# One expert choice spread over more vector slots, its counts copied out of PSUM first, and a row load put in front of twelve weight loads

## The chip, the cores and the metric

The kernel runs on one core of a Trainium2 chip. The metric is the device time of the whole program in microseconds (us): the median of three runs before the change is 731.31 us, from 730.92 to 732.39. A profile shows one further execution, in which TensorE (PE, with its weight loads PEld), VectorE (DVE), ScalarE (ACT), GpSimd (POOL) and SyncE (SP, here a queue that issues DMAs) each work through instructions of their own in order, and wait for one another on semaphores.

## The reference

Three stages follow one another; each is fp32.

```python
# clustered attention: 2 batches, 8 heads, 768 tokens, 64 columns
mask = q_assign[:, :, :, None] == k_assign[:, :, None, :]
scores = np.where(mask, scale * np.matmul(q, k.transpose(0, 1, 3, 2)), -1e9)
attn = softmax(scores);  x = attn @ v              # -> (1536, 512)
# mixture of experts: 8 experts, one expert per token
e_idx = np.argmax(x @ w_gate, axis=1)
h = np.maximum(x[mask_e] @ w1[e], 0.0)
out[mask_e] = gate_w * sigmoid(x @ w_output_gate)[e] * (h @ w2[e])
# dense feed-forward, 512 -> 2048 -> 512
h = x @ w_in;  g = h * sigmoid(1.702 * h);  return g @ w_out
```

## The kernel before, in words

**Attention.** The work is cut into eight units, one for a batch and a pair of heads (batch 0 is units 0 to 3, batch 1 units 4 to 7), and each unit into 12 steps of 128 queries against 768 keys, so 96 steps in one loop over `i`. In iteration `i` the program issues, in this order: the scores of step `i+1` on PE (L515 and L516, four matmuls in a PSUM tile `sp`, of which there are two) and their maximum on DVE (L518, `nm`); the piece of output that is due (L586, `pox`); what a table puts at this `i` (`soon_at`, below); the products with v (L567, only in some iterations, which makes those steps longer); the six transposes of step `i-1` (L532, `pt`, two groups of three: the first copied out by ACT at L537, the second by DVE at L539); last, the exponential of step `i+1` on ACT (L524, `P`). The scores of a step need two tiles in a row to come free, a transpose needs `P`, and `P` needs `nm`: PE, DVE and ACT work in a loop.

**Routing of a batch.** `route(gi)` is a generator: after each group of three transposes the loop advances it by two `yield`s (`advance(2)`), so four in an iteration. `route(0)` handles the 768 tokens of batch 0 while units 5 to 7 run. It finds each token's expert; ranks the tokens within their expert with matmuls into the PSUM tile `prk` (L652 to L661); and puts in the same bank, as `part`, the number of tokens of each expert. From `part` it chooses one expert, the one with most tokens (`soonh`), and sets aside up to 128 of its tokens (`ngone`, `gone`); it derives from that the addresses `dest` of all rows, then a gate value, and sends the rows to DRAM: per tile, a scaling on POOL (L725, `xs`) and an indirect DMA of POOL (L730, `xd`), one tile in an iteration, six in all.

**The PSUM bank `m`.** The pool `ps_m` has one bank. `prk` lies in it, and so do `pox` (L586), the transposed q and k of the next unit (`pqk`, L337) and cluster scores (`pcl`, L418). The tile after `prk` can be written when the last reader of `prk` is done.

**The early expert work.** The chosen expert's 128 rows are worked off in plain fp32 while the routing is finished. `soon_ids` (L747) loads the expert's number and first row into registers of SP; `soon_weights` issues twelve weight loads on SP (L760, `ew`, nine of 384 KB, two of 256 and one of 128); `soon_rows` issues the load of the 128 rows (L782, `xs`), behind a wait for all six scatters; `soon_x` transposes them on PE (L790, `pxs`) in iteration 91, and the matmuls with the weights (L806, L816) come behind the loop, once route(2) begins. `soon_at` sets the iterations of these four; SP works through its queue in the order in which they are issued. POOL also cuts the next unit's q and k in two parts for the scores (L343 and L344: `Hq`, `Lq`, `Hk`, `Lk`), and SP copies these to where the scores read them (L362).

Of the kernel before, what the change touches and what calls it, by code (L numbers as in the profile page):

```python
# [14 lines left out]
ALU = mybir.AluOpType  # L15
# [8 lines left out]
E = 8  # L24
# [22 lines left out]
def attention_moe_ffn(ctx: ExitStack, tc: tile.TileContext, q, k, v, centroids, w_gate, w_og, w1, w2, w_in, w_out, out):  # L47
    nc = tc.nc
# [11 lines left out]
    rev8 = const.tile([128, E], F32, name="rev8")  # L60
    ebase = const.tile([128, E], F32, name="ebase")
# [17 lines left out]
    soon = const.tile([1, 2], I32, name="soon")  # L79
    gone = const.tile([128, E], F32, name="gone")  # L80
    ngone = const.tile([128, 1], F32, name="ngone")
    sbase = const.tile([128, E], F32, name="sbase")
    srev8 = const.tile([128, E], F32, name="srev8")
    span = const.tile([128, 3], F32, name="span")
    soonh = const.tile([128, E], F32, name="soonh")
# [460 lines left out]
    def queue_av(i):  # L546
# [33 lines left out]
        def ostage():  # L580
            n = len(heads)
            hh = 2 * pr + heads[0]
            po = ps_m.tile([128, 512], F32, name="pox", tag="m")
            pv = po[:, :3 * n * XW].rearrange("p (r h c) -> p r h c", r=3, h=n)
            for r in range(3):
                nc.tensor.matmul(pv[:, r], hold["oa"][:, r * 128:(r + 1) * 128], wl[:, 2 * pr + h] if alone else wo[:, pr], start=True, stop=True)  # L586
            scale = hold["rs"][:, heads[0]:heads[-1] + 1].rearrange("p h r -> p r h")
            nc.vector.tensor_tensor(xw[b][:, j0:j0 + 3, hh:hh + n, :], pv, scale[:, :, :, None].to_broadcast([128, 3, n, XW]), op=ALU.mult)
            if (pr, j0) == (H // 2 - 1, 0) and b == B - 1:
                routing.append(route(1))  # L590
# [15 lines left out]
    def route(gi):  # L606

        b, j0, nj = GROUPS[gi]
        js = slice(j0, j0 + nj)

        def new(nm, shape, dt=F32):
            return one.tile(shape, dt, name=f"{nm}{gi}")
# [37 lines left out]
        rk = pr[:, :nj * E].rearrange("p (t e) -> p t e", t=nj)  # L650
# [7 lines left out]
        if gi < len(GROUPS) - 1:  # L658
            part = pr[:, 256:256 + E]
# [6 lines left out]
        dest = new("dest", [128, nj, E])  # L666
        if gi < len(GROUPS) - 1:
            lk = new("lk", [128, E])
        if gi == 0:
            nc.vector.scalar_tensor_tensor(lk, part, float(E), rev8, op0=ALU.mult, op1=ALU.add)  # L670
            lm, lv = new("lm", [128, 1]), new("lv", [128, E])
            nc.vector.tensor_reduce(lm, lk, op=ALU.max, axis=AX.X)
            nc.vector.tensor_scalar(soonh, lk, lm, None, op0=ALU.is_equal)
            yield
            nc.vector.tensor_tensor(lv, soonh, part, op=ALU.mult)
            nc.vector.tensor_reduce(ngone, lv, op=ALU.add, axis=AX.X)
            nc.vector.tensor_scalar(ngone, ngone, float(FIRST), None, op0=ALU.min)
            yield
            nc.vector.tensor_scalar(gone, soonh, ngone, None, op0=ALU.mult)
            nc.vector.scalar_tensor_tensor(sbase, gone, -1.0, ebase, op0=ALU.mult, op1=ALU.add)  # L680
            nc.vector.scalar_tensor_tensor(srev8, gone, -float(E), rev8, op0=ALU.mult, op1=ALU.add)
            yield
            nc.vector.tensor_tensor(lv, soonh, ebase, op=ALU.mult)
            nc.vector.tensor_reduce(span[:, 1:2], lv, op=ALU.add, axis=AX.X)
            nc.vector.tensor_tensor(span[:, 0:1], span[:, 1:2], ngone, op=ALU.subtract)
            yield
            nc.vector.tensor_tensor(lv, soonh, iota8, op=ALU.mult)
            nc.vector.tensor_reduce(lm, lv, op=ALU.add, axis=AX.X)
            nc.vector.tensor_copy(soon[:, 0:1], lm[0:1])
            nc.vector.tensor_copy(soon[:, 1:2], span[0:1, 0:1])  # L690
        nc.vector.tensor_tensor(dest, rk, sbase[:, None, :].to_broadcast([128, nj, E]), op=ALU.add)
        if gi == len(GROUPS) - 2:
            nc.vector.scalar_tensor_tensor(lk, part, float(E), srev8, op0=ALU.mult, op1=ALU.add)
        yield
# [13 lines left out]
        if gi == len(GROUPS) - 2:  # L708
            lm, lv = new("lm", [128, 1]), new("lv", [128, E])
# [40 lines left out]
    def soon_weights():  # L750

        m1_ = w1[bass.ds(sooner["e"], 1)].rearrange("o (k p) f -> p (o k) f", p=128)
        m2_ = w2[bass.ds(sooner["e"], 1)].rearrange("o (i p) d -> p (o i) d", p=128)
        homes = [(ld, f"ld_{nm}", 4 if nm == "v" else 2) for nm in "qqkkvv"] + [(one, x + nm, 1) for x in "HL" for nm in "qk"] + [(one, "Fq", 1)]

        def tile_of(*parts):
            pool, tag, bufs = homes.pop(0)
            t = pool.tile([128, 3, 256], F32, name="ew", tag=tag, bufs=bufs)
            for n, src in parts:
                nc.sync.dma_start(out=t[:, n:n + src.shape[1]], in_=src)  # L760
            return t
        cols = [slice(256 * c, 256 * c + 256) for c in range(4)]
        for c in range(4):
            t = tile_of((0, m1_[:, 0:3, cols[c]]))
            for k in range(3):
                sooner[1, k, c] = t[:, k]
        t = tile_of((0, m1_[:, 3, 0:768].rearrange("p (c f) -> p c f", c=3)))
        for c in range(3):
            sooner[1, 3, c] = t[:, c]
        t = tile_of((0, m2_[:, 6:8, cols[0]]), (2, m1_[:, 3:4, cols[3]]))  # L770
        sooner[2, 6, 0], sooner[2, 7, 0], sooner[1, 3, 3] = t[:, 0], t[:, 1], t[:, 2]
        yield
        for x in range(2):
            for i0 in (0, 3, 6)[:2 if x == 0 else 3]:
                t = tile_of((0, m2_[:, i0:min(i0 + 3, 8), cols[x]]))
                for i in range(i0, min(i0 + 3, 8)):
                    sooner[2, i, x] = t[:, i - i0]
        yield
# [139 lines left out]
    slots.update({21: 3, 27: 1, 75: 1, 80: 1, 81: 2, 86: 3, 87: 2, 92: 2, 93: 2})  # L918

    weights = soon_weights()  # L920
    soon_at = {75: [soon_ids], 84: [lambda: next(weights)], 87: [lambda: next(weights), soon_rows], 91: [soon_x]}

    fixed = ExitStack()
    fixed.enter_context(tc.manual_schedule())
# [14 lines left out]
    for i in range(NS + 2):  # L939
# [16 lines left out]
        if i == NS // 2 + 13:  # L956
            routing.append(route(0))
# [24 lines left out]
    while ost:  # L982
        ost.popleft()()
    advance()
    routing.append(route(2))
    advance()
    finish_routing()
# [334 lines left out]
    with tc.manual_schedule():  # L1322
# [14 lines left out]
        for g in range(G + 2):  # L1337
# [24 lines left out]
            if g >= 2:  # L1362
                g0, ht = hq.popleft()
                e0, c0 = divmod(g0, 8)
# [128 lines left out]
```

## Time and profile before

| what | us |
|---|---|
| median of three runs | 731.31 (730.92 to 732.39) |
| the profiled execution | 733.72 |
| its span, first to last instruction | 732.0 |
| PE busy in the span | 703.2 (96%) |
| DVE busy | 458.1 (63%) |
| ACT busy | 393.0 (54%) |
| POOL busy | 264.4 (36%) |

The profiled execution's own time is 1.7 us above its span, which is what lies around the first and the last instruction, and 2.4 us above the median of the runs. Times in the rows count from the first instruction. An idle time in square brackets stands ahead of the instruction and names what ended it. [...]

### The profile page before, as it was taken

The page shows a single profiled execution, that of the slowest core. Times are in us where ns is not written, and L with a number is a line of the kernel's source. Part 1 is how long each engine was busy: PE and PEld are TensorE (multiplying, and loading weights), DVE is VectorE, ACT ScalarE, POOL GpSimd, SP SyncE. Part 2 cuts the span into 40 slices and gives each one's busy share as a digit, 9 for nine tenths or more (in the row PEclk, how much of TensorE's full clock was granted, in tenths as well). Part 3 has the DMA queues.
Part 4 walks back from the last instruction along what each step waited for, and adds up shares of the span by engine and source line. Part 5 has one row for each costly group of instructions (what it writes and reads, how often), then busy time and mean ns, then how long its engine had stood idle before and what let it go on. Part 6 is the DMA issues. An engine that isn't in the chain of part 4 may idle for free.

```text
span 732.0 us, 12543 instructions
## 1 busy us (share of the span) xinstructions
PE 703.2 (96%) x4522; PEld 580.2 (79%) x4522; DVE 458.1 (63%) x886; ACT 393.0 (54%) x789; POOL 264.4 (36%) x219
## 2 busy tenths in 40 slices
PE   8999999998999898999999897999999999999996
PEld 6776776776866678999999887888888888888885
DVE  6969788889888774344554545687655657232322
ACT  7767675675666544556777676544534344222120
POOL 2230330312750013755978889222432212020202
PEclk8999999999899999999999999999999999999999
DMA  6778969637274427766477776132643211010101
GB/s 195 171 189 266 238 216 293 142 121 173 69 200 141 174 86 255 230 215 215 161 254 243 236 224 222 59 116 86 68 73 41 81 59 56 1 58 1 58 0 58
DMA packets 70594, 105.18 MB, mean 144 GB/s; under 512 B 9648, under 2 KB 48304, under 8 KB 70528
## 3 DMA queue, kind: packets, MB, share of 16 engines
q1 hardware_dynamic: 67584, 95.94, 45.9%
q0 software_dynamic: 2944, 8.40, 3.0%
q8 instruction: 37, 0.61, 0.4%
q14 instruction: 29, 0.24, 0.1%
HBM read 70.46 MB, written 14.69 MB: 116 GB/s over the span
## 4 chain that ended last, share of the span: by engine, by line
PE 33%; issue 16%; ACT 5%; DVE 3%; POOL 2%; DMA 1%; POOLq 0%; ACTq 0%; DVEq 0%
PE ph L1317 4%; PE ph L1318 4%; PE ph L1319 4%; PE py L1412 3%; PE py L1411 3%; PE py L1410 3%; PE py L1134 3%; ACT w L1048 3%; PE ph L1134 3%; PE ph L1135 1%; PE py L1135 1%; DVE w L1051 1%; DMA raw<-in_moe_w_dram 1%; POOL out_dram L1421 1%; ACT hs L1140 1%
## 5 line engine op out<-in xcount | busy, mean ns | idle before, releaser
L1051 POOL TENSOR_TENSOR w<-raw,w 128x1024 fp32r<-128x1024 f32 x51 | 125.6, 2482 | 39.3 <-ACT w L1048 38.9
L518 DVE TENSOR_REDUCE nm<-sp 128x1 f32<-128x768 f32 x96 | 91.6, 955 | 16.2 <-PE sp L516 14.1
L1395 DVE TENSOR_TENSOR sg<-ph,sg 128x512 f32<-128x512 f32 x48 | 33.2, 691 | 99.7 <-ACT sg L1394 97.5
L524 ACT ACTIVATE P<-sp,nm 128x768 f32<-128x768 f32 x96 | 87.2, 908 | 11.3 <-DVE nm L518 10.6
L532 PEld LDWEIGHTS pt<-ident,P 128*128 128x128 f32 x576 | 66.4, 143 | 28.1 <-issue 17.5
L532 PE MATMUL pt<-ident,P 128*128 128x128 f32 x576 | 84.3, 280 | 4.0 <-ACT pT L537 2.1
L1394 ACT ACTIVATE sg<-ph 128x512 f32<-128x512 f32 x48 | 28.7, 597 | 104.7 <-PE ph L1319 100.3
L1134 PE MATMUL py<-ht,w 128*128 128x512 f32 (+6 forms) x224 | 70.2, 367 | 8.0 <-DVE ht L1158 5.1
L515 PE MATMUL sp<-X,Q 128*128 128x384 f32 x192 | 74.9, 390 | 0.5 <-ACT P L524 0.4
L1412 PE MATMUL py<-w,gl 128*128 128x512 f32 (+1 forms) x194 | 75.2, 387 | 0.0
L1411 PE MATMUL py<-w,gh 128*128 128x512 f32 (+1 forms) x194 | 75.1, 387 | 0.0
L1410 PE MATMUL py<-w,gh 128*128 128x512 f32 (+1 forms) x194 | 75.0, 387 | 0.0
L1317 PE MATMUL ph<-yth,w 128*128 128x512 f32 x192 | 74.8, 390 | 0.0
L1318 PE MATMUL ph<-ytl,w 128*128 128x512 f32 x192 | 74.7, 389 | 0.0
L1319 PE MATMUL ph<-yth,w 128*128 128x512 f32 x192 | 74.7, 389 | 0.0
L1084 POOL TENSOR_TENSOR w<-csq,w 128x512 fp32r<-128x512 f32 x24 | 32.7, 1364 | 115.7 <-ACT w L1083 115.7
L1048 ACT CAST w<-raw 128x1024 fp32r<-128x1024 f32 x68 | 70.5, 1042 | 4.2 <-issue 2.4
L1134 PE MATMUL ph<-t,w 128*128 128x512 f32 (+6 forms) x224 | 69.4, 365 | 0.4 <-DVE ht L1158 0.4
L567 PE MATMUL po<-pT,ld_v 128*32 128x384 f32 x768 | 69.0, 492 | 0.0
L516 PE MATMUL sp<-Z,Q 80*128 80x384 f32 x192 | 66.4, 346 | 0.5 <-DMA Q<-ohT 0.5
L537 ACT COPY pT<-pt 128x384 f32<-128x384 f32 x96 | 45.8, 477 | 36.8 <-PE pt L532 36.8
L539 DVE COPY pT<-pt 128x384 f32<-128x384 f32 x96 | 52.8, 550 | 12.6 <-PE pt L532 12.2
(291 smaller groups left out, 1476.2 us busy)
## 6 DMA issues: line engine op xcount, KB each, us to landing
raw<-in_moe_w_dram SPq DMA_DIRECT2D x64, 512.0 KB, 4.5
raw<-in_moe_w_in_dram SPq DMA_DIRECT2D x16, 512.0 KB, 4.1
raw<-in_moe_w_out_dram SPq DMA_DIRECT2D x16, 512.0 KB, 4.8
xd<-zrow SPq DMA_DIRECT2D x8, 768.0 KB, 5.9
Q<-Hq SPq DMA_DIRECT2D x28, 192.0 KB, 2.7
ew<-in_moe_w_dram SPq DMA_DIRECT2D x9, 384.0 KB, 7.8
ld_q<-in_q_dram SPq DMA_DIRECT2D x8, 384.0 KB, 6.0
ld_k<-in_k_dram SPq DMA_DIRECT2D x8, 384.0 KB, 3.8
```

Source lines behind the costliest of these rows:

```text
L518: nc.vector.tensor_reduce(nm, sp[:, :, :384], op=ALU.max, axis=AX.XY, negate=True)
L524: nc.scalar.activation(P, L["sp"][:, :, :384], AF.Exp, bias=L["nm"], accum_out=L["sm"][:, h, j % 3:j % 3 + 1])
L532: nc.tensor.transpose(pt[:, r * 128:(r + 1) * 128], L["P"][:, n, r * 128:(r + 1) * 128], ident)
L1048: nc.scalar.copy(hi, r)
L1051: (eng or nc.gpsimd).tensor_tensor(lo, r, f32(hi), op=ALU.subtract)
L1134: nc.tensor.matmul(ps[:, :2 * n], w_hi, t, start=first, stop=False)
L1317: nc.tensor.matmul(ph, wa(key, 0, k, i), yth[:, k, cs], start=(k == 0), stop=False)
L1318: nc.tensor.matmul(ph, wa(key, 0, k, i), ytl[:, k, cs], start=False, stop=False)
L1319: nc.tensor.matmul(ph, wa(key, 1, k, i), yth[:, k, cs], start=False, stop=(k == 3))
L1410: nc.tensor.matmul(po[m][:, cs], gh[:, ms], wb(key, 0, i)[:, cs], start=first, stop=False)
L1411: nc.tensor.matmul(po[m][:, cs], gh[:, ms], wb(key, 1, i)[:, cs], start=False, stop=False)
L1412: nc.tensor.matmul(po[m][:, cs], gl[:, ms], wb(key, 0, i)[:, cs], start=False, stop=last)
```

## The change

Three things change, all for the first batch's choice.

In `route(0)` the addresses are now formed first, from the ranks and the full table of first rows (`ebase`), and the counts `part` are copied into a tile `c0`; behind that nothing reads `prk`. The operations of the choice follow with a `yield` after nearly each one, where there were two or three between two `yield`s, and `gone` is taken off the addresses at the end. That adds two vector operations (the copy, and the subtraction on 128x48) and moves all that stands behind: the gates and the six scatters.

`soon_ids` moves from iteration 75 to 78, `soon_rows` from 87 to 84, where it stands in front of the first seven weight loads.

```diff
         if gi == 0:
-            nc.vector.scalar_tensor_tensor(lk, part, float(E), rev8, op0=ALU.mult, op1=ALU.add)
-            lm, lv = new("lm", [128, 1]), new("lv", [128, E])
+            nc.vector.tensor_tensor(dest, rk, ebase[:, None, :].to_broadcast([128, nj, E]), op=ALU.add)
+            lm, lv, c0 = new("lm", [128, 1]), new("lv", [128, E]), new("c0", [128, E])
+            nc.vector.tensor_copy(c0, part)
+            yield
+            nc.vector.scalar_tensor_tensor(lk, c0, float(E), rev8, op0=ALU.mult, op1=ALU.add)
+            yield
             nc.vector.tensor_reduce(lm, lk, op=ALU.max, axis=AX.X)
+            yield
             nc.vector.tensor_scalar(soonh, lk, lm, None, op0=ALU.is_equal)
             yield
-            nc.vector.tensor_tensor(lv, soonh, part, op=ALU.mult)
+            nc.vector.tensor_tensor(lv, soonh, c0, op=ALU.mult)
+            yield
             nc.vector.tensor_reduce(ngone, lv, op=ALU.add, axis=AX.X)
+            yield
...
+            nc.vector.tensor_tensor(dest, dest, gone[:, None, :].to_broadcast([128, nj, E]), op=ALU.subtract)
+        else:
+            nc.vector.tensor_tensor(dest, rk, sbase[:, None, :].to_broadcast([128, nj, E]), op=ALU.add)
...
-    soon_at = {75: [soon_ids], 84: [lambda: next(weights)], 87: [lambda: next(weights), soon_rows], 91: [soon_x]}
+    soon_at = {78: [soon_ids], 84: [soon_rows, lambda: next(weights)], 87: [lambda: next(weights)], 91: [soon_x]}
```

What PE and ACT are given, and in which order, stays the same. Three queues change their order. On DVE, before, from the scaled first rows `sbase` to the last reader of `prk`, which is L691:

```order
L680 SCALAR_TENSOR_TENSOR sbase<-gone,ebase 128x8
L681 SCALAR_TENSOR_TENSOR srev_76<-gone,rev_63 128x8
L683 TENSOR_TENSOR lv_2579<-soonh,ebase 128x8
L684 TENSOR_REDUCE span<-lv_2579 128x1
L685 TENSOR_TENSOR span<-span,ngone 128x1
L518 TENSOR_REDUCE nm<-sp 128x1
L687 TENSOR_TENSOR lv_2579<-soonh,iota_65 128x8
L688 TENSOR_REDUCE lm_2578<-lv_2579 128x1
L689 CAST soon<-lm_2578 1x1
L690 CAST soon<-span 1x1
L691 TENSOR_TENSOR dest_2575<-prk,sbase 128x48
L695 TENSOR_TENSOR dest_2575<-dest_2575,roh_85 128x48
```

Now, in the same place of the program, from the operation that stood ahead of the choice (L664) on:

```order
L664 TENSOR_REDUCE z_2572<-zz_2543 128x6
L670 TENSOR_TENSOR dest_2575<-prk,ebase 128x48
L672 COPY c_2580<-prk 128x8
L674 SCALAR_TENSOR_TENSOR lk_2576<-c_2580,rev_63 128x8
L539 COPY pT<-pt 128x3x128
L676 TENSOR_REDUCE lm_2578<-lk_2576 128x1
L678 TENSOR_SCALAR soonh<-lk_2576,lm_2578 128x8
L518 TENSOR_REDUCE nm<-sp 128x1
L680 TENSOR_TENSOR lv_2579<-soonh,c_2580 128x8
L682 TENSOR_REDUCE ngone<-lv_2579 128x1
L539 COPY pT<-pt 128x3x128
L684 TENSOR_SCALAR ngone<-ngone 128x1
```

The last reader of `prk` stood 20 rows behind L664 and is now the second row behind it; between two operations of the attention (L539, L518) stand two of the choice, where six stood.

On POOL, before, the end of the six scatters (`xs`, `xd`) and the parts of the last unit's q and k:

```order
L343 CAST Hq<-Fq 128x384
L344 TENSOR_TENSOR Lq<-Fq,Hq 128x384
L725 TENSOR_SCALAR xs<-xw_114,gate_2649 128x512
L730 DMA xd<-xs,di_2627 12416x512
L733 ISA
L343 CAST Hk<-Fk 128x384
L344 TENSOR_TENSOR Lk<-Fk,Hk 128x384
L343 CAST Hk<-Fk 128x384
L344 TENSOR_TENSOR Lk<-Fk,Hk 128x384
L176 DMA wd<-csq 128x512
```

Now, the same place:

```order
L343 CAST Hk<-Fk 128x384
L344 TENSOR_TENSOR Lk<-Fk,Hk 128x384
L741 TENSOR_SCALAR xs<-xw_114,gate_2758 128x512
L746 DMA xd<-xs,di_2712 12416x512
L749 ISA
L343 CAST Hk<-Fk 128x384
L344 TENSOR_TENSOR Lk<-Fk,Hk 128x384
L741 TENSOR_SCALAR xs<-xw_114,gate_2758 128x512
L746 DMA xd<-xs,di_2712 12416x512
L749 ISA
L741 TENSOR_SCALAR xs<-xw_114,gate_2758 128x512
```

Of the six scatters all stood ahead of the last three parts or further up, four of them ahead of the first; now one stands ahead of the first part and two stand behind the last.

On SP, before, the end of the weight loads and the row load:

```order
L760 ISA
L760 DMA ew<-in_moe_w_dram 128x2x256
L782 ISA
L782 DMA xs<-xd 128x512
L1006 TENSOR_LOAD lead
```

Now, the start of them, behind the rows of one-hots (`ohT`) for the last unit:

```order
L435 DMA Q_2780<-ohT 16x384 x2
L798 ISA
L798 DMA xs<-xd 128x512
L776 ISA
L776 DMA ew<-in_moe_w_dram 128x3x256
```

The row load stood behind all twelve weight loads and stands ahead of them. Further up SP, the register loads of `soon_ids` now stand behind the load `raw<-in_moe_w_out_dram` (L113) instead of ahead of it.

## Rows read from the trace of the kernel before

**Rows 1.** Stages: us, busy us (count) of each engine, granted clock, DMA share, GB/s.
```profile
171.75:191.39 19.64, 17.38 (x125) 12.91 (x123) 17.50 (x56) 9.69 (x23) 5.57 (x5) 0.83 0.39 102
206.88:222.03 15.15, 14.07 (x117) 10.11 (x116) 14.32 (x24) 9.45 (x21) 4.15 (x6) 1.00 0.70 192
```

**Rows 2.** Timeline of the choice: start, us, engine, line, names [idle before, releaser].
```profile
178.58 0.19 DVE L664 TENSOR_REDUCE z<-zz 128x6 f32<-128x48 f32 x1
...
179.80 0.55 DVE L539 COPY pT<-pt 128x384 f32<-128x384 f32 x1
...
180.31 0.81 PE L532 MATMUL pt<-ident,P 128*128 128x128 f32 x3 [1.01 <-ACT pT L537]
...
181.23 0.96 DVE L518 TENSOR_REDUCE nm<-sp 128x1 f32<-128x768 f32 x1
...
182.62 0.18 DVE L691 TENSOR_TENSOR dest<-prk,sbase 128x48 f32<-128x48 f32 x1
...
182.86 1.97 PE L586 MATMUL pox<-wo,oa 128*128 128x160 f32 x6 [0.45 <-DVE dest L691]
...
185.76 0.67 PE L515 MATMUL sp<-X,Q 128*128 128x384 f32 x1
```

**Rows 3.** Timeline of DVE behind the choice: its idle times, first and last.
```profile
186.15 0.56 DVE L539 COPY pT<-pt 128x384 f32<-128x384 f32 x1 [0.53 <-PE pt L532]
...
189.74 0.55 DVE L405 TENSOR_TENSOR oh<-eq,m 128x384 bf16<-128x384 f32 x1
...
196.03 0.96 DVE L518 TENSOR_REDUCE nm<-sp 128x1 f32<-128x768 f32 x1 [0.22 <-PE sp L516]
```

**Rows 4.** Timeline of POOL: scatters and parts.
```profile
185.74 1.57 POOL L725 TENSOR_SCALAR xs<-xw,gate 128x512 f32<-128x512 f32 x1 [8.02 <-DVE gate L707]
...
188.78 1.58 POOL L725 TENSOR_SCALAR xs<-xw,gate 128x512 f32<-128x512 f32 x1
...
205.86 1.05 POOL L730 DMA_INDIRECT xd<-xs,di  x1 [0.28 <-POOL xs L725]
...
207.56 1.01 POOL L344 TENSOR_TENSOR Lk<-Fk,Hk 128x384 fp32r<-128x384 f32 x1
```

**Rows 5.** Timeline: one DVE operation in two units, and a PE wait behind it.
```profile
142.90 0.56 DVE L392 TENSOR_TENSOR eq<-sc,m 128x384 f32<-128x384 f32 x1
...
207.60 1.39 DVE L392 TENSOR_TENSOR eq<-sc,m 128x384 f32<-128x384 f32 x1
...
212.94 0.55 PE L532 MATMUL pt<-ident,P 128*128 128x128 f32 x3 [1.08 <-DVE pT L539]
```

**Rows 6.** Timeline of SP's queue: issue start, us taken by the issues.
```profile
213.29 0.77 SPq L362 DMA_DIRECT2D Z<-Hk  x1
217.02 0.35 SPq L113 DMA_DIRECT2D raw<-in_moe_w_out_dram  x1
223.98 1.21 SPq L435 DMA_DIRECT2D Z<-ohT  x2
...
229.19 4.61 SPq L760 DMA_DIRECT2D ew<-in_moe_w_dram  x7
...
239.66 0.34 SPq L782 DMA_DIRECT2D xs<-xd  x1
```

**Rows 7.** Timeline of PE around the transposes of the rows.
```profile
248.14 0.63 PE L790 MATMUL pxs<-ident,xs 128*128 128x128 f32 x4 [2.41 <-DMA xs<-xd]
...
249.62 0.67 PE L515 MATMUL sp<-X,Q 128*128 128x384 f32 x1
...
253.70 0.55 PE L532 MATMUL pt<-ident,P 128*128 128x128 f32 x3
```

**Rows 8.** Instructions of the weight tile: count, ns (min/median/max), first and last start.
```profile
L806 PE MATMUL pt<-xst,ew x64: 275/275/377, 267.3 to 276.3; 128*128 128x128 f32 x64
```

**Rows 9.** Stages behind the rows' wait and behind the routing, columns as in rows 1.
```profile
250.00:252.00 2.00, 2.00 (x12) 1.12 (x15) 1.20 (x2) 1.29 (x3) 0.00 (x0) 0.50 0.00 0
...
290.00:292.00 2.00, 2.00 (x10) 2.00 (x9) 0.33 (x1) 1.28 (x3) 2.00 (x2) 0.50 0.95 267
```

More of the change, by code (lines that the diff above doesn't have):

```diff
@@ L679, in route @@
             nc.vector.tensor_scalar(gone, soonh, ngone, None, op0=ALU.mult)
+            yield
             nc.vector.scalar_tensor_tensor(sbase, gone, -1.0, ebase, op0=ALU.mult, op1=ALU.add)
+            yield
             nc.vector.scalar_tensor_tensor(srev8, gone, -float(E), rev8, op0=ALU.mult, op1=ALU.add)
@@ L683, in route @@
             nc.vector.tensor_tensor(lv, soonh, ebase, op=ALU.mult)
+            yield
             nc.vector.tensor_reduce(span[:, 1:2], lv, op=ALU.add, axis=AX.X)
+            yield
             nc.vector.tensor_tensor(span[:, 0:1], span[:, 1:2], ngone, op=ALU.subtract)
             yield
+            nc.vector.tensor_copy(soon[:, 1:2], span[0:1, 0:1])
             nc.vector.tensor_tensor(lv, soonh, iota8, op=ALU.mult)
+            yield
             nc.vector.tensor_reduce(lm, lv, op=ALU.add, axis=AX.X)
+            yield
             nc.vector.tensor_copy(soon[:, 0:1], lm[0:1])
-            nc.vector.tensor_copy(soon[:, 1:2], span[0:1, 0:1])
-        nc.vector.tensor_tensor(dest, rk, sbase[:, None, :].to_broadcast([128, nj, E]), op=ALU.add)
+            yield
+            nc.vector.tensor_tensor(dest, dest, gone[:, None, :].to_broadcast([128, nj, E]), op=ALU.subtract)
+        else:
+            nc.vector.tensor_tensor(dest, rk, sbase[:, None, :].to_broadcast([128, nj, E]), op=ALU.add)
         if gi == len(GROUPS) - 2:
```

## The prediction, made before the changed kernel was run

> **What bounds the kernel now.** I read the stages first [rows 1]. Over the span PE is busy for 96%, but two stretches of the attention are not what PE needs. Two stretches of six steps each lie one unit apart and are alike in all but the routing: 206.88 to 222.03 takes 15.15 us, 171.75 to 191.39 takes 19.64. [...] DVE is busy 17.50 of its 19.64 us. The reader is to see that 4.5 us are lost here, and that DVE has little to spare.
>
> Then I read the timeline [rows 2] for what ends PE's waits there. At 180.31 a group of transposes had waited 1.01 us; its PSUM tile comes free by the vector copy at 179.80, which stood behind the choice's first six operations. At 182.86 the output matmuls L586 had waited 0.45 for L691, the last reader of the bank `m`. Transposes, scores and output then run at the low clock. The exponential also waits for its maximum, which starts at 181.23, long after its scores. From 186 on DVE idles between its operations, six times, from 0.53 at 186.15 to 0.22 at 196.03 [rows 3], 2.3 us in all: PE leads again.
>
> Last come PE's rows at the end of the attention [rows 7] with SP's queue [rows 6]. PE stops for 2.41 us before the transposes of the 128 rows. Their load was issued at 239.66, behind twelve weight loads begun at 229.19, so it landed 8.5 us after its issue. At 250 to 252 the clock is 0.50 [rows 9].
>
> **Part 1: the choice spread out, its bank left early.** Nothing changes up to L664 (178.58). I then walk the new order of DVE with spacings from start to start of the old one: 0.2 us for a small operation that needs the one before, 0.1 for one that doesn't, 0.46 for a copy, 0.87 for a maximum. The two readers of `prk` start at 178.7 and 178.8; the bank is free at 178.95, where L691 ended at 182.80. The copy of 179.80 starts at 179.1 with one small operation ahead instead of six. So the transposes of 180.31 start at 179.65 and their wait falls from 1.01 to 0.35. The maximum of 181.23 starts at 179.95. The output matmuls of 182.86 follow their scores at 180.84 and wait for no one. The scores of 185.76 start at 182.5: 3.2 us earlier, a good part of it because PE keeps 2.4 GHz.
>
> Then DVE pays. Some twenty small operations of the choice, the addresses and the gate come now in what was 186 to 196. Twenty by 0.19 is 3.8 us, where 2.3 us were idle, and with PE 3 us ahead that idle time is also what shrinks. Two of them are new: the copy of counts and the subtraction, 0.16 and 0.2 by their likes (L691, 0.18 [rows 2]). Walking on, DVE is full up to the maximum of 196.03, which now starts at 193.2, and PE's transposes there wait about 0.4 for it. I end with a lead of 2.6 us, and carry that: **2.6 us**.
>
> Its bounds: at most the 4.5 us by which the stretch exceeds its like, and by DVE's 17.50 busy of 19.64 less the operations moved out of it hardly over 3.2. At least 0.7: that is the same walk with the clock falling as before, where PE's six steps stay slow and only the waits of 1.01 and 0.45 shrink, to about half.
>
> POOL follows the gate, whose end started the scatters at 185.74 [rows 4]. The new gate starts at 192.7. A scatter takes 3.0 us (185.74 to 188.78), a pair of parts 1.6 (1.01 of it L344). With the order of the change: scatter, parts, scatter, parts, scatter, parts (205.1), scatter (206.6), parts (209.6 to 211.2), two scatters to 217.2; the last was issued at 205.86 before. The last parts feed copies that SP ends about 215, and the last unit needs them only behind the one-hot rows that SP issued from 223.98 on [rows 6]: some 6 us of cover at the new times. Their price without it is one for one.
>
> The later POOL work may also meet DVE. In the last unit L392 took 1.39 us beside POOL's L344 at 207.56, in an earlier one, with POOL idle, 0.56 [rows 5]. That 0.8 remains: the parts of k and L392 move about alike, 2 and 2.6 us earlier. Between never meeting (-1.0) and meeting once more (+0.8) I take 0. The scalings cost nothing: L405 at 189.74 took 0.55 wholly within a scaling from 188.78 to 190.36 [rows 3, 4].
>
> [...]
>
> **Part 2: the row load in front.** PE's scores end at 248.14 - 2.41 = 245.73, and the four transposes of the rows can follow. The rows' load leaves SP ahead of the weights, at about 229.2 - 2.6 = 226.6, when the last scatter (217.2) is 9 us old. Even with the 8.5 us that it took in the crowd it would land at 235; PE asks at 243. So the wait goes. Behind it, the scores at 249.62 then start at 246.8, and the transposes of 253.70 at 249.75, since products and scores run at 2.4 GHz: **3.95 us**. From 250 to 252 DVE is busy for 1.20 us, PE for all 2.00, so PE is what ends last there. Bounds: 2.4, if the clock falls by itself, to 4.0.
>
> The weights are delayed by one issue, 0.35 us [rows 6], and 256 KB. They are used first at 267.3 [rows 8], some 28 us after their last issue at 239: covered. The register loads of `soon_ids` took about 3 us (214.06 to 217.02) ahead of a load; behind it they must end before 223.98: covered by 4 us at the new times as well, else up to 3 us.
>
> What follows the attention starts from routing on DVE and from registers loaded behind it, and so shifts as a whole.
>
> **Sum.** 2.6 + 3.95 = 6.55 us. The profiled execution: 733.72 - 6.55 = 727.2 (span 725.5). The runs shown have a median 2.4 lower, so 731.31 - 6.55 = **724.8 us**.
>
> **Rivals.**
> First: the clock falls in the choice all the same, or DVE's queue takes back the lead by 197. For it: DVE is 89% busy there, and the small rank matmuls before 178 stay. Against: a wait of 1.08 at 212.94 [rows 5] left the clock at 1.00 throughout [rows 1], and the waits after the change are shorter. Part 1 is 0.7: 731.31 - 4.65 = 726.7.
>
> [...]
>
> Second: the gain is partly given back behind the routing. At 290 to 292 the clock is 0.50 [rows 9] after PE's thin stretch of transposes there; if that low stretch were 3 us longer, half of it, 1.5, would go. [...] Against: no load or wait there starts from anything that doesn't shift. 731.31 - 6.55 + 1.5 = 726.3.
>
> Third, slower: the row load stops SP. It waits for six scatters that now end later, and all weights, the later loads and the register for the next experts queue behind it. It costs nothing until the rows land after 243, then one for one; beyond 249.7 the kernel is slower than before. The last scatter would have to take over 30 us to land. At 252 it would give 731.31 + 2.3 = 733.6. Nothing in the rows speaks for it but that the landing of a scatter is not shown.
>
> Fourth: the bank is freed early, but PE's loop was held by DVE alone, and part 2's wait passes to another late piece: 731.31 - 0.7 = 730.6.
>
> **How the numbers follow.** Forecast 0.60, its own range 723.0 to 726.0; first rival 0.20; second 0.12; third 0.04; fourth 0.04. The range for 8 in 10 runs from 722.6 (DVE and POOL meeting no more, part 1 at its upper end) to 728.6 (the first two rivals together, with some tenths for the unknown meetings). A measurement of this kernel tells about 0.2%, 1.5 us, from no change: faster 0.92, within 0.04, slower 0.04.
>
> **What would show it.** Right: L586 no longer waits for the routing's vector work; the clock holds near 1.00 from 176 to 190; L588 precedes the choice's later operations; the row transposes have no wait for a DMA and the clock stays up behind; the first L806 starts about 6.5 us earlier. Wrong: transposes that wait a microsecond for L539 around 190 to 197 (DVE's queue); L392 or L135 well over 1.4; a low clock near 180; an SP wait at the row load.

## The result and the profile after

The changed kernel took 725.44 us (median of 4 runs, 723.91 to 726.63), the kernel before 731.85 in the same session (730.92 to 732.95): a ratio of 0.9907, 95% interval 0.9885 to 0.993. Run again with the later experiments it took 725.51 us, ratio 0.9909 (0.9892 to 0.9925). The forecast was 724.8.

The profiled execution took 726.63 us, with a span of 724.9 (732.0 before). Behind the choice a line's number is 16 higher than before: L725, L730, L760, L782 and L790 are now L741, L746, L776, L798 and L806.

To see where the time went, I compare the start of the first L516 (the scores) of a step in both traces; of each stretch between two such starts the table shows the length in us.

| stretch | before | after | gained |
|---|---|---|---|
| start of the span to step 66 (in front of the choice) | 178.28 | 179.11 | -0.83 |
| step 66 to 70 (the choice) | 13.37 | 9.85 | +3.52 |
| step 70 to 76 (addresses and gate) | 15.51 | 15.41 | +0.10 |
| step 76 to 83 (one-hots of the last unit) | 18.73 | 18.02 | +0.71 |
| step 83 to 85 (first scores of the last unit) | 3.12 | 4.27 | -1.15 |
| step 85 to 92 | 16.04 | 16.04 | 0.00 |
| step 92 to 95 (transposes of the rows) | 13.14 | 8.97 | +4.17 |
| step 95 to the end of the span | 473.8 | 473.3 | +0.6 |

The sum is 7.1, the difference of the spans. The first and the last line differ by more than that from one execution to another whatever the edit (below), so I take the 7.35 between them as the change's own.

**The choice.** These stages of the kernel after answer to the first of [rows 1], to the stage behind it and to the first of [rows 9]; columns as there.

```profile
172.57:188.69 16.12, 14.42 (x124) 10.30 (x123) 15.64 (x49) 9.65 (x23) 0.56 (x1) 1.00 0.37 106
188.69:204.10 15.41, 15.41 (x137) 11.63 (x136) 12.54 (x28) 10.59 (x25) 9.90 (x9) 1.00 0.23 67
...
250.00:252.00 2.00, 2.00 (x21) 1.36 (x14) 1.75 (x6) 1.09 (x3) 0.47 (x1) 1.00 0.03 8
```

The reader is to see that the stage fell by 3.52 us, and of what: PE's busy time fell from 17.38 to 14.42 with the same work (125 and 124 instructions recorded), which is 2.96; what PE stood idle fell by 0.56 only. The granted clock, a share of TensorE's full speed, is 1.00 where it was 0.83 as a mean: before, it was 0.50 from 181 to 187. So most of the gain against this execution is not the waits themselves but the clock of 1.00 that PE kept. DVE is busy for 15.64 of 16.12 us. In the next stage 28 operations stand on DVE, where 18 stood (191.39 to 206.88 of the kernel before), and PE is busy all the time nonetheless.

The timeline of the kernel after, of DVE and PE in the choice, answers to [rows 2] and [rows 3]:

```profile
179.52 0.20 DVE L670 TENSOR_TENSOR dest<-prk,ebase 128x48 f32<-128x48 f32 x1
179.63 0.16 DVE L672 COPY c<-prk 128x8 f32<-128x8 f32 x1
...
179.91 0.55 DVE L539 COPY pT<-pt 128x384 f32<-128x384 f32 x1
...
180.51 0.55 PE L532 MATMUL pt<-ident,P 128*128 128x128 f32 x3 [0.38 <-DVE pT L539]
...
181.61 0.98 PE L586 MATMUL pox<-wo,oa 128*128 128x160 f32 x6
...
189.13 0.20 DVE L705 TENSOR_TENSOR dest<-dest,gone 128x48 f32<-128x48 f32 x1
189.36 0.21 DVE L711 TENSOR_TENSOR dest<-dest,roh 128x48 f32<-128x48 f32 x1
189.49 0.19 DVE L713 TENSOR_REDUCE es<-df 128x6 f32<-128x48 f32 x1
189.60 0.55 DVE L539 COPY pT<-pt 128x384 f32<-128x384 f32 x1
...
193.46 0.95 DVE L518 TENSOR_REDUCE nm<-sp 128x1 f32<-128x768 f32 x1
...
195.04 0.96 DVE L518 TENSOR_REDUCE nm<-sp 128x1 f32<-128x768 f32 x1 [0.17 <-PE sp L516]
```

The bank is free at 179.79, where the copy of the counts ends (179.63 + 0.16), in front of the next copy of transposes. The wait of 1.01 is 0.38, the wait of L586 is gone, and its six matmuls take 0.98 us where they took 1.97. The maximum that began at 196.03 begins at 193.46, though this execution came to the choice 0.83 later; the first idle time of DVE behind the choice stands at 195.04, where the first stood at 186.15.

**The rows.** Timeline of the kernel after, of SP's queue and PE; it answers to the last of [rows 6] and to [rows 7].

```profile
226.89 0.38 SPq L798 DMA_DIRECT2D xs<-xd  x1
...
243.24 0.60 PE L806 MATMUL pxs<-ident,xs 128*128 128x128 f32 x4
...
244.25 0.42 PE L515 MATMUL sp<-X,Q 128*128 128x384 f32 x1
...
247.19 0.88 PE L532 MATMUL pt<-ident,P 128*128 128x128 f32 x6
```

No wait for the DMA is left, and 250 to 252 has a clock of 1.00 (first fence).

**A wait that I had not foreseen.** Timeline of the kernel after where the last unit begins: POOL, SP's queue, PE.

```profile
215.33 1.70 SPq L113 DMA_DIRECT2D raw<-in_moe_w_out_dram  x1
216.51 1.02 POOL L746 DMA_INDIRECT xd<-xs,di  x1 [0.28 <-POOL xs L741]
217.56 0.61 POOL L176 DMA_DIRECT2D wd<-csq  x1
...
221.75 2.13 SPq L435 DMA_DIRECT2D Q<-ohT  x2
...
225.19 0.44 PE L516 MATMUL sp<-Z,Q 80*128 80x384 f32 x1 [1.25 <-DMA Q<-ohT]
```

The one-hot rows were not issued late: the issue at 221.75 is 3.49 us earlier than its like before (225.24, last fence here), as much as PE came earlier. But the pair of issues took 2.13 us where it had taken 1.21, and the rows landed after PE asked. The stages of the kernel after, and then of the kernel before, over the same 12 us:

```profile
214.00:218.00 4.00, 4.00 (x38) 2.33 (x38) 3.77 (x7) 2.94 (x7) 3.62 (x4) 1.00 0.96 245
218.00:222.00 4.00, 4.00 (x39) 2.36 (x40) 3.29 (x8) 2.34 (x5) 0.17 (x1) 1.00 0.82 266
222.00:226.00 4.00, 2.75 (x20) 2.43 (x19) 2.17 (x4) 2.92 (x7) 0.00 (x0) 1.00 0.19 52
```

```profile
214.00:218.00 4.00, 4.00 (x30) 3.73 (x29) 3.62 (x6) 3.15 (x7) 0.00 (x0) 1.00 0.74 213
218.00:222.00 4.00, 4.00 (x39) 2.34 (x38) 3.72 (x6) 2.43 (x7) 0.00 (x0) 1.00 0.37 133
222.00:226.00 4.00, 4.00 (x39) 2.36 (x38) 3.17 (x7) 2.81 (x7) 0.00 (x0) 1.00 0.06 14
```

Timeline of SP's queue in the kernel before:

```profile
225.24 1.21 SPq L435 DMA_DIRECT2D Q<-ohT  x2
```

The share of the DMA engines (second column from the right) is 0.82 in the stretch in which the issues of the one-hot rows begin; before, they began at 223.98 [rows 6], at a share of 0.06. The last scatters and the transfer of csq behind them, all issued by POOL, and the weights `raw`, issued by SP, now run up to there: from 218 to 222 the queue that carries POOL's transfers (`q0`) takes 29% of the engines' time and the one that carries SP's (`q1`) 53%. That the full engines made the rows late is what this suggests; the experiments below test it.

### The profile page after: what moved, and what is told of

Its sections match the earlier page's. It is cut to its first block, busy times and chain, and to the rows that moved or that the text cites. A ratio compares the mean times of both kernels' runs of the same rounds, so it can differ in the third digit from the quotient of the medians.

```text
span 724.9 us, 12544 instructions
## 1 busy us (share of the span) xinstructions
PE 698.2 (96%) x4522; PEld 576.5 (80%) x4522; DVE 457.4 (63%) x888; ACT 392.5 (54%) x789; POOL 263.8 (36%) x219
## 4 chain that ended last, share of the span: by engine, by line
PE 36%; issue 16%; ACT 4%; DVE 3%; POOL 1%; POOLq 0%; ACTq 0%; DVEq 0%
PE py L1150 4%; PE ph L1333 4%; PE ph L1335 4%; PE ph L1334 4%; PE ph L1150 3%; PE py L1428 3%; PE py L1427 3%; PE py L1426 3%; ACT w L1064 3%; PE py L1151 2%; PE ph L1151 2%; DVE w L1067 1%; POOL out_dram L1437 1%; ACT hs L1156 1%; DVE ph L1157 1%
## 5 line engine op out<-in xcount | busy, mean ns | idle before, releaser
L518 DVE TENSOR_REDUCE nm<-sp 128x1 f32<-128x768 f32 x96 | 91.6, 955 | 15.2 <-PE sp L516 14.1
L515 PE MATMUL sp<-X,Q 128*128 128x384 f32 x192 | 73.4, 382 | 0.4 <-ACT P L524 0.4
L516 PE MATMUL sp<-Z,Q 80*128 80x384 f32 x192 | 65.4, 341 | 1.8 <-DMA Q<-ohT 1.8
L539 DVE COPY pT<-pt 128x384 f32<-128x384 f32 x96 | 52.7, 549 | 8.1 <-PE pt L532 7.8
```

The costliest lines, as they stand in the source:

```text
L518: nc.vector.tensor_reduce(nm, sp[:, :, :384], op=ALU.max, axis=AX.XY, negate=True)
```

## The experiments

The stretches of the table above, as what each kernel gained on the kernel before in its own profiled execution; the last column is the median of its runs and the ratio to runs of the kernel before on the same chip, with its interval.

| kernel | 66-70 | 70-76 | 76-83 | 83-85 | 92-95 | us; ratio |
|---|---|---|---|---|---|---|
| after | 3.52 | 0.10 | 0.71 | -1.15 | 4.17 | 725.44; 0.9907 (0.9885 to 0.993) |
| choice only | 3.52 | 0.11 | 0.71 | 0.00 | -0.33 | 730.07; 0.9948 (0.9925 to 0.997) |
| rows only | 0.45 | 0.09 | 0.28 | 0.00 | 4.17 | 728.52; 0.9924 (0.9901 to 0.9947) |
| bank only | 1.16 | 0.11 | 0.55 | -0.01 | 4.18 | 728.83; 0.993 (0.9905 to 0.9954) |
| six more | 3.54 | -0.15 | 0.65 | -0.01 | 4.17 | 725.1; 0.9889 (0.9864 to 0.9913) |
| after again | 3.52 | 0.11 | 0.70 | -1.19 | 4.17 | 725.51; 0.9909 (0.9892 to 0.9925) |
| ids at 75 | 3.52 | 0.10 | 0.69 | -0.26 | 4.17 | 726.18; 0.9919 (0.9901 to 0.9938) |
| scatters closer | 3.52 | 0.10 | 0.31 | -5.16 | 4.18 | 732.75, one run; none |
| scatters apart | 3.52 | 0.09 | 0.28 | -0.01 | 4.18 | 726.13; 0.991 (0.9896 to 0.9925) |

What lies in front of step 66 moved from -0.83 to +1.33 between these executions, and what lies behind step 95 took 472.7 to 474.9 us. The kernel before was run again beside each set: 734.44 us beside the kernels from choice only to six more, 732.80 beside the last four. The times in the expectations start from 731.9, so they are to be read as gains. With so much movement the medians don't add up as the stretches do.

**Choice only.** The table of `soon_at` as before, the choice as after.

```diff
-    soon_at = {78: [soon_ids], 84: [soon_rows, lambda: next(weights)], 87: [lambda: next(weights)], 91: [soon_x]}
+    soon_at = {75: [soon_ids], 84: [lambda: next(weights)], 87: [lambda: next(weights), soon_rows], 91: [soon_x]}
```

Expected: 

> Only the choice is spread and leaves PSUM early; the row load stays behind the weights and the register loads where they were. My theory, two separate gains: the step at 191.65 in the kernel before gains 3.5 us against the steps ahead of the choice, as in the changed kernel, and the clock stays at 1.00 from 176 to 190; PE still stops some 2.4 us before the row transposes and the clock falls behind it. If the wait of 1.25 us at the first scores of the last unit (new in the changed kernel) comes from the later scatters alone, it is here too: about 731.9 - 3.5 - 0.7 + 1.4 = 729.1 us. If it comes from the moved register loads, it is absent and the time is about 727.7. Rival: the vector queue takes the lead back, 731.

The choice alone gives the whole 3.52, and nothing is lost at step 84. Timeline of PE in this kernel: the wait for the rows stays, at the later load.

```profile
243.81 1.09 PE L806 MATMUL pxs<-ident,xs 128*128 128x128 f32 x4 [2.75 <-DMA xs<-xd]
```

**Rows only.** The choice as before, `soon_at` as after.

```diff
-    soon_at = {75: [soon_ids], 84: [lambda: next(weights)], 87: [lambda: next(weights), soon_rows], 91: [soon_x]}
+    soon_at = {78: [soon_ids], 84: [soon_rows, lambda: next(weights)], 87: [lambda: next(weights)], 91: [soon_x]}
```

Expected: 

> Only the order of the early expert loads: the row load in front of the weights, the register loads three iterations later; the choice as before. My theory: PE's 2.4 us before the row transposes go and the clock stays up behind, 4.1 us, and nothing else moves, as the scatters are as early as before: 731.9 - 4.1 = 727.8 us, with no wait at the first scores of the last unit. Rival, the moved register loads cause that wait: it is here, and the time is about 729.2. Rival, the wait passes to another late piece: 730 or more.

Timeline of PE in the choice, then its stage:

```profile
179.74 0.55 PE L532 MATMUL pt<-ident,P 128*128 128x128 f32 x3 [1.02 <-ACT pT L537]
...
182.29 1.69 PE L586 MATMUL pox<-wo,oa 128*128 128x160 f32 x6 [1.28 <-DVE dest L691]
```

```profile
171.18:190.36 19.18, 16.09 (x125) 11.86 (x123) 17.55 (x56) 9.68 (x23) 5.12 (x5) 0.91 0.40 104
```

The same order as before, and yet 0.45 faster in the choice: the clock fell only around L586 (1.00 from 180 to 182, 0.65 from 182 to 184, 0.50 from 184 to 186), not at the transposes, so PE's busy time is 16.09 (17.38 before). But L586 waits longer, 1.28 instead of 0.45. With PE quicker the wait for DVE grows: DVE is what ends last there. So the old choice has two sizes here, and against this one the new choice gains 3.06 us in its stage (19.18 to 16.12) instead of 3.52: 1.67 of PE's busy time and 1.39 of its idle time. The rows give 4.17, as in the whole change.

**Bank only.** `soon_at` as after; the bank is read and left at once, but the choice has its old few `yield`s.

```diff
+            nc.vector.tensor_tensor(dest, rk, ebase[:, None, :].to_broadcast([128, nj, E]), op=ALU.add)
...
+            nc.vector.tensor_copy(c0, part)
+            nc.vector.scalar_tensor_tensor(lk, c0, float(E), rev8, op0=ALU.mult, op1=ALU.add)
...
+            nc.vector.tensor_tensor(dest, dest, gone[:, None, :].to_broadcast([128, nj, E]), op=ALU.subtract)
```

Expected: 

> The changed kernel with the bank left early (addresses first, counts copied out), but the choice's operations in blocks of two to four between two slots, as in the kernel before; so the scatters are as early as before. My theory, the spread is what keeps PE fed and the clock up: transposes near 180 still wait about 1.0 us for a vector copy, the clock falls there, only the 0.45 us of the output matmuls and what hangs on it goes, a lead of about 1 us at the step of 191.65; no wait at the last unit's first scores; 731.9 - 1.0 - 4.1 = 726.8 us. Rival, the bank was all: a lead of 3.5 us at that step, the clock at 1.00, and 731.9 - 3.5 - 4.1 = 724.3 us.

Timeline of PE in the choice, then its stage:

```profile
180.53 0.90 PE L532 MATMUL pt<-ident,P 128*128 128x128 f32 x3 [1.01 <-ACT pT L537]
...
182.51 1.50 PE L586 MATMUL pox<-wo,oa 128*128 128x160 f32 x6
```

```profile
171.97:190.45 18.48, 16.04 (x125) 11.69 (x123) 17.74 (x58) 9.79 (x23) 4.46 (x4) 0.91 0.37 107
```

L586 waits for no one, but the wait of 1.01 and the low clock behind it stay: 1.16 of 3.52, and against rows only, which shares the rest, 0.7. So the larger part comes with the spreading, by either measure of the old choice. The spreading without the early bank was not tried: the bank's last reader would stand behind a maximum whose scores PE issues behind L586, which waits for that reader.

**Six more.** The kernel after, with six copies of 128x8 on DVE in the choice that nobody reads.

```diff
+            pad = [new(f"pad{i}", [128, E]) for i in range(3)]
+            for i in range(2):
+                nc.vector.tensor_copy(pad[i % 3], ebase)
...
```

Expected: 

> The changed kernel with six more small vector copies (128x8) of no use between the choice's later operations, two in each of three slots, at 0.1 to 0.2 us each, 0.6 to 1.2 us in all. If the vector queue is what bounds the stretch from 180 to 197 (the vector engine busy 1.93 to 2.00 of every 2 us there), the steps from the one at 191.65 on come 0.6 to 1.2 us later than in the changed kernel: about 726.3 us. If PE bounds it by then, they come 0 to 0.2 later: 725.5.

Stages of this kernel, as the first two of the kernel after:

```profile
170.41:186.53 16.12, 14.44 (x125) 10.32 (x123) 15.67 (x55) 9.68 (x23) 0.56 (x1) 1.00 0.42 107
186.53:202.17 15.64, 15.64 (x137) 11.63 (x135) 12.83 (x28) 10.66 (x25) 9.89 (x9) 1.00 0.22 65
```

Six operations more, 55 for 49, and the stage is as long; the next is 0.23 longer. That is 0.04 us for one, where 0.1 to 0.2 was expected, and the 0.23 lies just above what was expected if PE bounds the stretch.

**After again, ids at 75, scatters closer, scatters apart.** These four look at the wait at step 84. After again is the changed kernel unaltered. Ids at 75 moves only the register loads back. The other two set how many `yield`s stand in front of each scatter's next, four in the changed kernel, to two (closer, the second diff) or six (apart, with `range(5 ...)` in the same line):

```diff
-    soon_at = {78: [soon_ids], 84: [soon_rows, lambda: next(weights)], 87: [lambda: next(weights)], 91: [soon_x]}
+    soon_at = {75: [soon_ids], 84: [soon_rows, lambda: next(weights)], 87: [lambda: next(weights)], 91: [soon_x]}
```

```diff
-            for _ in range(3 if gi == 0 else 0):
+            for _ in range(1 if gi == 0 else 0):
```

Expected of after again: 

> The changed kernel once more, unaltered, beside the three next. Theory: the lead of 3.5 us at step 70 and of 4.2 us at the row transposes come again, since nothing in them hangs on when a transfer starts. The wait of PE at the first scores of the last unit (1.25 us on the one-hot rows, step 84) is a size of that one execution: it was 0.4 in the kernel with six added operations, whose SP and POOL order is the same, so here anything from 0.3 to 1.4. Rival: it belongs to the order and is 1.1 to 1.4 again. About 725.4 us, 6.4 below before, by either, 0.5 less where the wait is short.

Timeline of PE in this kernel:

```profile
223.90 0.44 PE L516 MATMUL sp<-Z,Q 80*128 80x384 f32 x1 [1.27 <-DMA Q<-ohT]
```

The wait came again, within the rival's 1.1 to 1.4; the stretches repeat to 0.04 us. But in six more, with the same order of SP and POOL, PE does not wait there: 0.01 lost. (The 0.4 that the expectation gives for it is the idle time of PE's weight loads ahead of that matmul, 0.35, not of PE.) So the order alone doesn't decide. Nor does the share of the DMA engines. Stages that end 0.5 to 1.2 us ahead of step 83, in after again (1.19 lost), choice only (0.00) and six more, then PE at step 84 in six more:

```profile
218.00:220.00 2.00, 2.00 (x26) 0.68 (x24) 1.75 (x4) 1.15 (x3) 0.00 (x0) 1.00 0.91 338
218.00:220.00 2.00, 2.00 (x26) 0.68 (x24) 1.75 (x4) 1.27 (x3) 0.00 (x0) 1.00 0.90 291
218.00:220.00 2.00, 2.00 (x27) 0.80 (x20) 1.97 (x4) 0.82 (x2) 0.00 (x0) 1.00 0.91 353
...
222.18 0.45 PE L516 MATMUL sp<-Z,Q 80*128 80x384 f32 x1
```

The engines are as full in all three, so a mean share of 0.9 does not tell whether the rows land in time.

Expected of ids at 75: 

> Only the register loads go back to iteration 75, ahead of the weights for the second expert matmul, which then start some 2 to 3 us later (217 instead of 214 to 215). Theory (the late one-hot rows come of too many transfers in 214 to 221, and the expert weights that now start early are a part of them): the wait at step 84 is at most 0.3, and the span is up to 1.1 us shorter than that of a run of the changed kernel with a wait of 1.25. Rival (the late scatters and the load of csq behind them alone fill the transfer engines): the wait stays what it is in e8, and the time is that of e8. Nothing else moves: lead at step 70 of 3.5.

Timeline of SP's queue and PE:

```profile
216.51 0.35 SPq L113 DMA_DIRECT2D raw<-in_moe_w_out_dram  x1
...
222.80 0.45 PE L516 MATMUL sp<-Z,Q 80*128 80x384 f32 x1 [0.35 <-DMA Q<-ohT]
```

The wait is 0.35 (the theory had at most 0.3) with `raw` issued 2.5 us later than in after again. That speaks for the theory, and so does choice only, with `raw` at 216.65 and 0.00 lost. It is not shown by this, since six more lost only 0.01 with the early `raw`. The medians tell nothing: the ratios, 0.9919 and 0.9909, lie within each other's intervals.

Expected of scatters closer: 

> Two yields in front of each scatter's next instead of four, so a scatter comes twice as often between the parts of the last unit's q and k. Theory of the cover: POOL's last part ends about 217 instead of 211, SP's copies of it end about 219 to 221 instead of 215, and the issue of the one-hot rows behind them moves from 222 to 224 or 225: the cover of 6 us is used up, and PE's wait at the first scores of the last unit grows to 2.5 to 4 us, so 727 to 729 us. Rival (the cover is larger than the 6 us, since the wait there is set by the one-hot rows alone): the wait is as in e8, or none because the scatters are done earlier, and the time is that of e8. The lead at step 70 stays 3.5, as the scatters start behind it.

Timeline of POOL and PE, then stages:

```profile
216.57 1.01 POOL L344 TENSOR_TENSOR Lk<-Fk,Hk 128x384 fp32r<-128x384 f32 x1
...
227.95 0.69 PE L516 MATMUL sp<-Z,Q 80*128 80x384 f32 x1 [4.00 <-DMA Q<-ohT]
```

```profile
228.00:230.00 2.00, 2.00 (x8) 1.90 (x9) 0.61 (x1) 0.04 (x1) 0.00 (x0) 0.50 0.16 41
...
232.00:234.00 2.00, 2.00 (x10) 1.96 (x9) 1.43 (x2) 0.00 (x0) 0.00 (x0) 0.50 1.05 306
234.00:236.00 2.00, 2.00 (x16) 1.97 (x15) 1.35 (x3) 1.77 (x4) 0.00 (x0) 0.95 0.84 251
```

The wait is the 4 us that the theory had as its upper end, but the price is not: step 83 to 85 lost 5.16 and step 85 to 92 another 1.65, 6.8 us in all, since PE came out of the wait at a clock of 0.50 and stayed there for 6 us, from 228 to 234. Here the one-hot rows were issued late, as the theory said: the first at 224.76, behind the later copies, `raw` and the register loads, when step 83 had begun at 222.40. By the stretches 1.3 us of the gain is left between step 66 and 95; the one run, 732.75, can't tell that from the kernel before. The place of the scatters alone can use up most of the gain.

Expected of scatters apart: 

> Six yields in front of each scatter's next instead of four: the parts of the last unit pass ahead of more scatters, and the last two scatters stand behind the load of csq. Theory: the last part ends some 3 us earlier (about 208), SP's copies and the one-hot rows are issued earlier, the wait at step 84 is at most 0.2, and the last scatter ends about 222, still 5 us ahead of the row load's issue at 227: 0.3 to 1.1 us faster than e8. Rival: the transfers only spread to 214 to 225 and the late scatters meet the one-hot rows and the expert weights there, so the wait at step 84 stays or grows, or the rows of the early expert land later than 243 and PE waits at their transposes: not faster than e8, up to 2 us slower.

Stages where the one-hot rows are issued, then the timeline of DVE and POOL 12 us earlier:

```profile
214.00:218.00 4.00, 4.00 (x38) 2.32 (x37) 3.50 (x7) 2.46 (x6) 2.60 (x2) 1.00 0.80 253
218.00:222.00 4.00, 4.00 (x39) 2.35 (x38) 3.27 (x8) 2.83 (x6) 0.00 (x0) 1.00 0.21 68
```

```profile
205.90 1.01 POOL L344 TENSOR_TENSOR Lk<-Fk,Hk 128x384 fp32r<-128x384 f32 x1
206.04 1.42 DVE L135 SCALAR_TENSOR_TENSOR csq<-csq,ct 128x512 f32<-128x512 f32 x1
206.89 2.00 POOL L741 TENSOR_SCALAR xs<-xw,gate 128x512 f32<-128x512 f32 x1
```

The DMA share is 0.21 where it was 0.82, and PE does not wait: 0.01 lost. But 0.4 of it is given back between step 76 and 83, where L135 takes 1.42 us (0.67 before) beside the parts of k. What is left in the attention against after again, 0.7 us or 0.1%, the runs can't tell: 726.13 beside 725.51. No version measurably better than the changed kernel came of the experiments.

## Why the prediction was right, and where its steps were not

**The forecast's mechanism holds.** The bank leaves early, L586 waits for no one, the clock is 1.00 throughout the stage, the wait for the rows is gone. The first rival (the clock falls all the same) and the fourth are out in every one of the seven executions with the new choice, with 3.52 to 3.54 each time. The second rival, a longer low clock behind the routing, did not come in the changed kernel: the low clock stands at 284 to 286 (0.51) instead of 290 to 292 [rows 9], and the stretch from step 95 to the end is 473.3 us where it was 473.8. It is no idle fear, though: in rows only the clock there is 0.50 from 282 to 286, the matmuls L1130 to L1132 take 0.46 us each up to 288.2 and 0.30 behind it, and that stretch took 474.9. The third did not come: the row load was issued at 226.89 without holding up SP.

**Part 1 was mis-sized.** "Then DVE pays" was the step that failed: I took 3.2 us in the choice and gave 0.6 back behind it; measured were 3.52 and then +0.10. Against the old choice as rows only ran it, the two come to 3.06 and 0.01: the 3.2 is between the two sizes, and what was wrong by either is the 0.6 given back. The term was "twenty by 0.19 is 3.8 us". The fence above shows why 0.19 is too much: L711, L713 and the copy behind them start 0.13 and 0.11 apart. In these rows an operation has 0.2 us before the next only where the next needs its result at once, as L711 needs that of L705 (0.23). With an operation of the attention behind every one or two of the choice, most of that time is filled. The seventeen small operations from 184.05 to 193.03 take 1.93 us from start to start of what follows, 0.11 each, and the six copies of the experiment cost 0.04 each. So DVE had room for them, the lead stayed, and the upper bound of 3.2 was no bound: it counted DVE's busy time moved out, while DVE could be filled from 17.50 of 19.64 to 15.64 of 16.12.

What the gain is made of was right in kind: 2.96 of 3.52 is PE's own work at a mean clock of 1.00 instead of 0.83, or 1.67 of 3.06 (1.00 instead of 0.91) against rows only. No run shows the GHz in which the prediction puts the clock: the traces show a share of full speed, 1.00 throughout the new choice and 0.50 at the lowest in the old one. How long the clock falls in the old choice differs from one execution to the next (a mean of 0.83 in the kernel before, 0.91 in rows only and bank only); that it does not fall in the new one, 1.00 from 176 to 190, is the same in all seven.

**Part 2** was 3.95 by the sum and 4.17 or 4.18 by the traces of all eight executions that have it: the 2.41 of the wait, and 1.76 for the stretch at the low clock, of which I had counted 1.54. The weights came in time: the last was issued at 237.6, L822 used the first at 260.8, and no matmul on them waited for a DMA.

**The order of POOL and SP was costed at nothing, and cost 1.15 in this execution.** The times were right: the last parts, the copies and the last scatter came where the prediction had them. The cover of "some 6 us" was a cover for the issue of the one-hot rows alone; that they must also land, through DMA engines that the same moves had filled (a share of 0.82 from 218 to 222, 0.37 before), I did not cost. I also counted the move of `soon_ids` only for what stands behind it, not for `raw`, which it lets go 2 to 3 us earlier. The later POOL work is part of the cause: rows only and bank only, with the register loads at 78 too but the scatters early, lost 0.00 and 0.01; scatters apart, whose last scatter is as late (issued at 216.24) but whose csq and `raw` go 6.0 and 3.2 us earlier than in after again, lost 0.01. But with the scatters where the changed kernel has them the loss was 1.15, 1.19 and 0.01 with the register loads at 78, and 0.26 and 0.00 with them at 75. What decides between these, and what share the early `raw` has, stays open. Where I did price the cover's loss, "one for one" was too little: in scatters closer 4.00 us of wait cost 6.8.

**The meeting of L392 and L344** was taken as 0 between -1.0 and +0.8. It gave 0.7, the stretch from step 76 to 83. Timeline of DVE, POOL and PE in the kernel after, answering to [rows 5]:

```profile
204.82 0.70 DVE L392 TENSOR_TENSOR eq<-sc,m 128x384 f32<-128x384 f32 x1
...
207.14 1.56 POOL L741 TENSOR_SCALAR xs<-xw,gate 128x512 f32<-128x512 f32 x1
208.01 0.67 DVE L135 SCALAR_TENSOR_TENSOR csq<-csq,ct 128x512 f32<-128x512 f32 x1
...
209.48 0.55 PE L532 MATMUL pt<-ident,P 128*128 128x128 f32 x3 [0.50 <-DVE rs L577]
```

L392 took 0.70 instead of 1.39, and PE's wait fell from 1.08 to 0.50. In scatters apart and in rows only L392 takes 0.56, and L135 meets a part instead (1.42 and 1.24 us); there the stretch gains only 0.28. It is a matter of tenths, and of where POOL's parts fall.

In the last fence of scatters apart L135 ends at 207.46, 0.55 behind the end of L344 at 206.91, and the scaling that began at 206.89, beside it, takes 2.00 us instead of 1.57. But where a scaling began first, the vector operation was no longer: L135 took its 0.67 wholly within the scaling of 207.14 (last fence), as L405 had taken its 0.55 in [rows 3] and [rows 4]. Why the scaling took longer when L135 came first stays open.

**The sum** was 6.55; the traces give 7.35 in the attention (3.52 + 0.10 + 0.71 - 1.15 + 4.17), the medians 6.4 and 7.3. Part 1 was 1 us too small (0.5 against the old choice of rows only), the meeting 0.7 and part 2 0.2, and the wait that I had not seen took 1.15 of these back. That the forecast of 724.8 is nearer to 725.44 than its terms were to theirs is luck. The low end of the range, 722.6, does not follow from the two terms named for it: no meeting (1.0) and part 1 at 3.2 (0.6 more) give 723.2.

## What to carry to other kernels

A burst of small dependent operations held up a loop here by more than they cost when spread: the first six of the old choice, from 178.69 to the copy of 179.80, took 0.19 us each from start to start, and spread between the loop's own operations seventeen took 0.11 each. Where such a burst stands on an engine that shares a loop, try it spread. When a stage holds a fall of the clock, compare PE's busy time before and after as well as its waits, and profile the kernel before more than once: here the idle time gave 0.6 us and the busy time 3.0 against one execution of the old choice, 1.4 and 1.7 against another. And when work is moved to a later place, price the transfers that it starts by where they will meet others, until they land and not only until they are issued.

## What the runs showed that I had not expected

- A wait of 4.00 us was followed by 6 us at a clock of 0.50, so it cost 6.8; waits of 1.25 and 1.27 at the same place left the clock at 1.00 from 222 to 226. In rows only the clock stood at 1.00 behind a wait of 1.02 (180 to 182) and fell around one of 1.28 that ended 2.5 us later (0.50 from 184 to 186); in the kernel before it fell at a wait of 1.01 (0.73 from 180 to 181, 0.50 from 181 to 187), and in bank only at one of 1.01 too (its transposes behind it take 0.90 us, those of rows only 0.55). The waits of 1.01 and 1.02 with opposite ends show that the length of the wait alone did not decide; what did is not shown.
- Some issues of a DMA on SP's queue took longer than before: the pair of Q<-ohT 2.13 us from 221.75, with a DMA share of 0.78 from 220 to 222 and 0.22 from 222 to 224 (1.21 before, 0.06 from 222 to 226), and `raw` 1.70 from 215.33, with 0.96 from 214 to 218 (0.35 before [rows 6], 0.74). A high share alone did not do it: in ids at 75 `raw` took 0.35 at 216.51, with 0.96 from 216 to 218.
- With the change, the choice and the transposes of the rows repeat between executions to 0.03 us, while what lies in front and behind moves by 2 us each. Without it, where the clock falls, they don't: the choice took 13.37 and 12.91 us, the transposes of the rows 13.14 and 13.47. Leads measured within the trace told apart what intervals of 0.2% on the whole could not.
